# Last token pair of a down projection: the gate row folded into the last product's weight sums

## Chip, core and metric
The kernel runs on one core of one Trainium2 chip. The metric is the device time of one execution in microseconds (us). A core has five engines that run side by side: TensorE (PE, matmuls; PEld is its weight load), VectorE (DVE), ScalarE (ACT), GpSimd (POOL) and SyncE (SP, which here issues the DMAs). Matmul results go to PSUM, in eight banks of 512 f32 columns by 128 partitions; everything else lies in SBUF.

## What is computed
A transformer block on 2048 tokens of width 1024: linear attention, then a gated feed-forward network (hidden width 3584), each with a layer norm that is modulated by a condition vector and each added back through a gate row.

```
x = x + ga * attention(norm(x) * (1 + ca) + sa)
h = norm(x) * (1 + cb) + sb
x = x + gb * ((gelu(h @ w_gate) * (h @ w_up)) @ w_down)
```

The case lies in the last factor: `y @ w_down`, with y of 2048 x 3584, then the gate row gb (1024 numbers, one for each output column) and the sum with x. The output is bf16.

## The kernel before
One Python function records every instruction through a small scheduler (`sch.op`, `sch.dma`), which works out the semaphores from the byte ranges that each instruction reads and writes. Instructions run on each engine in the order in which they were recorded. A reordering by costs (`sch.reorder`) is applied to the part between the two marks, which ends before the down projection: in the part of this case the order is the one written by hand. A write of a range waits for its last TensorE reader, matmul by matmul.

The down projection goes by eight **token pairs** j of 256 tokens. A pair's product is seen as 2 x 2 blocks: token halves s (128 tokens each), halves l of each pair of the 28 hidden chunks, and output halves c (512 columns each). Instead of eight block products it takes **seven**, of sums of blocks (a Strassen-type scheme). Each of the seven is fourteen matmuls (NST = 14, k = 0 to 13): stationary operand 128 x 128 of activations, moving operand 128 x 512 of weights. The weights' sums (`TT[k][0..4]`, tiles named bt) were made once for all pairs, on VectorE (L1585) and ScalarE. The activations' sums (`XS[0]`, `XS[1]`, tiles named xs) are made for each pair from the loaded y (`YL`, tiles named yl): by `a_sum` on VectorE (L1613, in two halves of seven chunks each, `halves(i)`), the last as a copy on ScalarE (L1607).

The order for a pair is product 1, 5, 6, 2, 7, 3, 4 (`dprod`, whose matmuls are all recorded at L1619). Between them:
- `dpcp` (L1653, ScalarE) copies product 1 to bank BB, on which products 6, 7 and 4 are then summed up; `descp` (L1657, ScalarE) copies product 5 to SBUF.
- `halves(0)` must come before product 5, `halves(1)` before 6, `halves(2)` before 7, `halves(3)` before 3, and the copy of L1607 before 4. Products 5, 7 and 4 use XS[0], products 6 and 3 XS[1], so each sum also waits for the product that read the buffer before.
- `dpadd(j, BC)` (L1661, VectorE) reads bank BB after product 6 and before product 7; `dpadd(j, BE)`, after product 7 and before product 4.
- `devac(j, n)` evacuates a finished block n: VectorE multiplies the bank by the gate row GB16 in place (L1684), adds x from the slot `SLT` into the slot (L1685), and SyncE issues the store (L1686). Block 0 is ready after product 2, block 2 after the second `dpadd`, block 1 after product 3, block 3 (second 128 tokens, first 512 columns, bank BB) after product 4. Block 3 of a pair is evacuated during the next pair.

For the last pair, j = 7, nothing follows that could hide the evacuation of block 3. There product 4 covers 448 columns only. The last 64 columns are computed by `plain`, without sums, as 28 matmuls of 64 columns into the other BB bank; the evacuation is then in two parts, 448 and 64 columns, each a multiplication, a sum and a store.

GpSimd has no instruction in the down projection. Its last ones are the 128x1 steps of the second layer norm (L703, L707, L708, L710).

Of the kernel before, what the change touches and what calls it, by code (L numbers as in the profile page):

```python
# [8 lines left out]
ALU = mybir.AluOpType  # L9
# [55 lines left out]
NKP = NFP  # L65
NST = 14
# [30 lines left out]
OFF_SLOT = [OFF_ROW + 2048, OFF_ROW + 3072, OFF_GAB, OFF_GAB + 1024, OFF_GAB + 2048, OFF_GAB + 3072, OFF_GUH + 7168]  # L97
# [251 lines left out]
def bass_adaLN_cond__linear_attn_block__geglu_ffn__prompt_kernel(  # L349
# [18 lines left out]
    with ExitStack() as es:  # L368
# [6 lines left out]
        def at(name, shape, dty, off):  # L375
            return nc.alloc_sbuf_tensor_at(name, shape, dty, offset=ABASE + off, align_bytes=4)
# [21 lines left out]
        GB16 = at("gb16", [P, D], bf16, OFF_GB16)  # L398
        BXT = [at(f"bx{k}", [P, 2, 512], bf16, PB[k]) for k in range(NKP)]
        STT = [at(f"wst{k}", [P, 2, 512], bf16, PS2[k]) for k in range(NKP)]  # L400
        TT = [[at(f"bt{k}_{i}", [P, 512], f32r, PT[k][i]) for i in range(5)] for k in range(NST)]
        SLT = [at(f"x1s{i}", [P, 512], bf16, o) for i, o in enumerate(OFF_SLOT)]
# [59 lines left out]
        def r_sm(name):  # L462
            return [(SMO[name], SMO[name] + SMSZ[name], name)]
# [30 lines left out]
        def r_wv(g):  # L494
            return [(OFF_WK + g * 2048, OFF_WK + (g + 1) * 2048, "wv")]
# [64 lines left out]
        def r_bt(k, i):  # L560
            return [(PT[k][i], PT[k][i] + 2048, f"bt{k}_{i}")]

        def r_slot(i):
            return [(OFF_SLOT[i], OFF_SLOT[i] + 1024, f"x1s{i}")]
# [6 lines left out]
        R_GB16 = [(OFF_GB16, OFF_GB16 + 2048, "gb16")]  # L571
# [4 lines left out]
        def pr(b):  # L576
            return [(b * 2048, (b + 1) * 2048)]

        def PS(b, c0=0, c1=512):
            return ps_all[:, b * 512 + c0: b * 512 + c1]  # L580
# [4 lines left out]
        sch = Sched()  # L585
        T, A, V, G, Q = PE_, ACT_, DVE_, POOL_, SP_
# [3 lines left out]
        out_v = out[0].rearrange("(c p) d -> p c d", p=P)  # L590
# [60 lines left out]
        for q in range(1, 4):  # L651
            wmq_dma(q)
            for d0, d1 in ((2 * q, 2 * q + 1), (2 * q + 1, 2 * q + 2)):
# [8 lines left out]
               rd=r_sm("c8") + r_sm("ident"), pwr=pr(4))  # L662
# [4 lines left out]
               rd=r_sm("thc") + r_sm("chalf"), wr=r_sm("siluT"))  # L667
# [509 lines left out]
        for c_ in range(10, NCH):  # L1177
            b = seq.index(("k", c_ // 2 * 2, 0)) - (9 if c_ % 2 else 12)
# [6 lines left out]
        for c_ in range(8, NCH, 2):  # L1185
            b = seq.index(("k", c_, 0)) - 3
# [10 lines left out]
        for g in range(NG):  # L1197
            task(nk + g // 2, lambda g=g: sch.dma(Q, lambda e: e.dma_start(WV[:, g, :, :], wqkv_v[:, :, 2 * D + g * P:2 * D + (g + 1) * P]),
                                                  wr=r_wv(g), note=f"wv{g}"))
# [246 lines left out]
        BA, BE, BB, BC = 0, 2, 4, 6  # L1446
# [128 lines left out]
        TTF = [[t_.ap().bitcast(f32) for t_ in r_] for r_ in TT]  # L1575
# [23 lines left out]
        def a_sum(i, k0, k1, sh=0):  # L1599
            if k1 <= k0:  # L1600
                return
            lo = lambda s: YL[0][:, k0:k1, s * P:(s + 1) * P]
            hi = lambda s: YL[1][:, k0:k1, s * P:(s + 1) * P]
            x = lambda n: XSF[n][:, k0:k1, :]
            rl, rh = (lambda s: r_yl(0, k0, k1, s * P, (s + 1) * P)), (lambda s: r_yl(1, k0, k1, s * P, (s + 1) * P))
            if i == 4:
                sch.op(A, lambda e: e.activation(XS[0][:, k0 + sh:k1 + sh, :], hi(1), ACTF.Copy), rd=rh(1), wr=r_xq(0, k0 + sh, k1 + sh), note=f"acp.{k0}", overwrite_ok=True)  # L1607
                return
            d, in0, in1, op, rd = ((0, lo(1), hi(1), ALU.add, rl(1) + rh(1)),
                                   (1, x(0), lo(0), ALU.subtract, r_xq(0, k0, k1) + rl(0)),  # L1610
                                   (0, lo(0), lo(1), ALU.subtract, rl(0) + rl(1)),
                                   (1, hi(0), x(1), ALU.subtract, rh(0) + r_xq(1, k0, k1)))[i]
            sch.op(V, lambda e: e.tensor_tensor(XS[d][:, k0:k1, :], in0, in1, op), rd=rd, wr=r_xq(d, k0, k1), note=f"asum{i}.{k0}", overwrite_ok=True)  # L1613
# [13 lines left out]
        def dprod(j, i, k0, k1, n=512):  # L1627
            t, ks = j % 2, range(k0, k1)
            if i in (1, 2):
                lhs = [ya(i - 1, 0, k) for k in ks]  # L1630
                rhs = [(BXT[k][:, i - 1, :], r_bx(k, i - 1, i)) for k in ks]
            else:
                xi, ti = {5: (0, 0), 6: (1, 1), 7: (0, 2), 3: (1, 3), 4: (0, 4)}[i]
                sh = NEA if j == 0 and i == 4 else 0
                lhs = [(XS[xi][:, k + sh, :], r_xq(xi, k + sh, k + sh + 1)) for k in ks]
                rhs = [(TT[k][ti][:, 0:n], r_bt(k, ti)) for k in ks]
            b = {1: BA, 2: BA, 5: BE, 6: BB, 7: BB, 4: BB, 3: BC}[i] + t
            dmm(b, i in (1, 5) and k0 == 0, lhs, rhs, f"down j{j} P{i}", 0, n)

        def plain(j, s, c, k0, k1, b=None, c0=0, c1=512):  # L1640
            if b is None:
                b, fresh = ((BA, BC), (BB, BE))[s][c] + j % 2, False
            else:
                fresh = True
            w = (BXT, STT)[c]
            r = (r_bx, r_st)[c]
            lhs = [ya(l, s, k) for k in range(k0, k1) for l in range(2)]
            rhs = [(w[k][:, l, c0:c1], r(k, l, l + 1)) for k in range(k0, k1) for l in range(2)]
            dmm(b, fresh, lhs, rhs, f"down j{j} C{s}{c}", 0 if fresh else c0, c1 - c0 if fresh else c1)

        def dpcp(j):
            t = j % 2
            sch.op(A, lambda e: e.activation(PS(BB + t), PS(BA + t), ACTF.Copy), prd=pr(BA + t), pwr=pr(BB + t), note="pcp")  # L1653
# [5 lines left out]
        def dpadd(j, dst):  # L1659
            t = j % 2  # L1660
            sch.op(V, lambda e: e.tensor_tensor(PS(dst + t), PS(BB + t), ES[0][:, :], ALU.add), prd=pr(BB + t), rd=r_2k(OFF_ES[0], "es0"),  # L1661
                   pwr=pr(dst + t), note="padd")

        def tok(j):
            return (j // 4) * 8 + 2 * (j % 4)

# [9 lines left out]
        def devac(j, n, c0=0, c1=512, b=None):  # L1676
            s, c = TORD[n]
            i, c_ = (4 * j + n) % 7, tok(j) + s
            if b is None:
                b, p0, p1 = ((BA, BC), (BB, BE))[s][c] + j % 2, c0, c1  # L1680
            else:
                p0, p1 = 0, c1 - c0
            rng = [(OFF_SLOT[i] + c0 * 2, OFF_SLOT[i] + c1 * 2, f"x1s{i}")]
            sch.op(V, lambda e: e.tensor_tensor(PS(b, p0, p1), PS(b, p0, p1), GB16[:, c * 512 + c0:c * 512 + c1], ALU.mult), prd=pr(b), pwr=pr(b), rd=R_GB16, note=f"x2a {j}.{n}")  # L1684
            sch.op(V, lambda e: e.tensor_tensor(SLT[i][:, c0:c1], PS(b, p0, p1), SLT[i][:, c0:c1], ALU.add), prd=pr(b), rd=rng, wr=rng, note=f"x2b {j}.{n}")  # L1685
            sch.dma(Q, lambda e: e.dma_start(out_v[:, c_, c * 512 + c0:c * 512 + c1], SLT[i][:, c0:c1]), rd=rng, note=f"out{c_}.{c}.{c0}")  # L1686

        mark.append(sch.n)
        def cb1():
# [42 lines left out]
        for n in range(8):  # L1732
            i, j = divmod(n, 2)
# [4 lines left out]
        for n in range(4 * NEA):  # L1738
            v, k = 14 + (n + 1) // 2, (7, 1)[n % 2]
# [35 lines left out]
        def halves(i):  # L1775
            a_sum(i, 0, H)
            a_sum(i, H, NST)
# [40 lines left out]
        for j in range(1, NP):  # L1818
            lastj = j == NP - 1
            dprod(j, 1, 0, NST)  # L1820
            dpcp(j)
            if j == 1:
                devac(0, 0)
            else:
                halves(0)
                halves(1)
                devac(j - 1, 3)
            x1_load(j, 3)
            dprod(j, 5, 0, NST)
            descp(j)  # L1830
            halves(2)
            if not lastj:
                y_load(j + 1, 0)
            if j == 1:
                devac(0, 1)
            dprod(j, 6, 0, NST)
            dpadd(j, BC)
            halves(3)
            if j == 1:
                devac(0, 2)  # L1840
            dprod(j, 2, 0, NST)
            devac(j, 0)
            if not lastj:
                x1_load(j + 1, 0)
            dprod(j, 7, 0, NST)
            dpadd(j, BE)
            a_sum(4, 0, H)
            if not lastj:
                y_load(j + 1, 1, 0, H)
            a_sum(4, H, NST)  # L1850
            if not lastj:
                y_load(j + 1, 1, H, NKP)
            devac(j, 2)
            if j == 1:
                devac(0, 3)
            if not lastj:
                x1_load(j + 1, 1)
            dprod(j, 3, 0, NST)
            devac(j, 1)
            if not lastj:  # L1860
                x1_load(j + 1, 2)
            if not lastj:
                dprod(j, 4, 0, NST)
            else:
                dprod(j, 4, 0, NST, 448)
                plain(j, 1, 0, 0, NKP, b=BB + 1 - j % 2, c0=448, c1=512)
                devac(j, 3, 0, 448)
                devac(j, 3, 448, 512, b=BB + 1 - j % 2)


        sch.reorder(mark[0], mark[1], (DVE_, ACT_, POOL_), {id(x4_op): 8.0})
# [73 lines left out]
```

## Time and profile before

| what | us |
|---|---|
| median of 3 runs (lowest, highest) | 786.57 (786.21, 787.83) |
| the profiled execution | 786.67 |
| its span, first to last instruction | 784.9 |
| PE busy | 777.6 (99%) |
| DVE busy | 644.6 (82%) |
| ACT busy | 347.3 (44%) |
| POOL busy | 44.5 (6%) |
| last pair's matmuls (product 1 to the 64 column piece) | 759.14 to 781.84 |
| last DMA issue | 782.90 to 783.29 |

Times "at" are counted from the span's start. The granted TensorE clock is 1.00 over the whole span. Busy shares are means over stages; the change lies in the last 3% of the span, so its own stretch has to be read. A matmul's length in the trace includes its way through the array, and matmuls overlap: the distance from start to start is what one costs.

### The profile page before, as it was taken

The page shows a single profiled execution, that of the slowest core. Times are in us where ns is not written, and L with a number is a line of the kernel's source. Part 1 is how long each engine was busy: PE and PEld are TensorE (multiplying, and loading weights), DVE is VectorE, ACT ScalarE, POOL GpSimd, SP SyncE. Part 2 cuts the span into 40 slices and gives each one's busy share as a digit, 9 for nine tenths or more (in the row PEclk, how much of TensorE's full clock was granted, in tenths as well). Part 3 has the DMA queues.
Part 4 walks back from the last instruction along what each step waited for, and adds up shares of the span by engine and source line. Part 5 has one row for each costly group of instructions (what it writes and reads, how often), then busy time and mean ns, then how long its engine had stood idle before and what let it go on. Part 6 is the DMA issues. An engine that isn't in the chain of part 4 may idle for free.

```text
span 784.9 us, 11098 instructions
## 1 busy us (share of the span) xinstructions
PE 777.6 (99%) x3897; PEld 498.7 (64%) x3897; DVE 644.6 (82%) x1082; ACT 347.3 (44%) x584; POOL 44.5 (6%) x126
## 2 busy tenths in 40 slices
PE   8999999999999999999999999999999999999998
PEld 4444445666445667677777767677776576777766
DVE  6699989993498987888999988898988897676775
ACT  2497743333474476766645444444545011111111
POOL 2031300000230011010000000000000000000000
PEclk9999999999999999999999999999999999999999
DMA  9789749826596377555455567555536445344341
GB/s 283 254 168 249 158 93 255 220 69 115 134 256 188 90 230 236 155 148 148 120 145 170 143 182 207 162 162 150 153 100 182 123 127 162 119 141 138 111 141 35
DMA packets 210544, 125.94 MB, mean 160 GB/s; under 512 B 70572, under 2 KB 200116, under 8 KB 210488
## 3 DMA queue, kind: packets, MB, share of 16 engines
q1 hardware_dynamic: 210472, 125.23, 58.8%
q8 instruction: 31, 0.51, 0.3%
q14 instruction: 25, 0.20, 0.1%
q10 hardware_dynamic: 16, 0.00, 0.0%
HBM read 88.35 MB, written 23.22 MB: 142 GB/s over the span
## 4 chain that ended last, share of the span: by engine, by line
PE 94%; DMA 3%; SPq 2%; DVE 1%; issue 0%; ACT 0%; DVEq 0%; ACTq 0%
PE ps_all L1468 45%; PE ps_all L1619 23%; PE ps_all L1303 7%; PE ps_all L969 7%; PE ps_all L933 6%; PE ps_all L918 5%; DMA mtb<-mb 1%; DMA wmq<-in_w_mod_dram 1%; SPq L631 1%; SPq L636 0%; DMA h1T<-xh 0%; PE ps_all L951 0%; PE ps_all L1234 0%; PE ps_all L1261 0%; SPq L625 0%
## 5 line engine op out<-in xcount | busy, mean ns | idle before, releaser
L1468 PE MATMUL ps_all<-ss,tp 128*128 128x512 f32 x896 | 224.9, 403 | 0.0
L1468 PEld LDWEIGHTS ps_all<-ss,tp 128*128 128x128 f32 x896 | 167.8, 188 | 41.1 <-DVE ps_all L1480 0.7
L1485 ACT ACTIVATE ge<-ps_all 128x512 f32<-128x512 f32 x112 | 66.8, 597 | 133.1 <-DVE ps_all L1480 82.3
L1619 PE MATMUL ps_all<-bt,xs 128*128 128x512 f32 (+1 forms) x520 | 123.8, 395 | 0.0
L1619 PEld LDWEIGHTS ps_all<-bt,xs 128*128 128x128 f32 x520 | 97.6, 188 | 22.2 <-DVE ps_all L1661 0.5
L1489 DVE TENSOR_TENSOR yr<-ge,ps_all 128x512 bf16<-128x512 f32 x112 | 76.7, 685 | 30.5 <-PE ps_all L1468 14.4
L1480 DVE TENSOR_TENSOR ps_all<-ps_all,es 128x512 f32<-128x512 f32 x112 | 72.4, 692 | 7.8 <-PE ps_all L1468 6.9
L1442 DVE TENSOR_TENSOR tp<-wt 128x512 fp32r<-128x512 bf16 x112 | 72.1, 685 | 1.3
L1442 DVE TENSOR_TENSOR tp<-wt,tp 128x512 fp32r<-128x512 bf16 x112 | 72.1, 685 | 0.0
L1619 PE MATMUL ps_all<-bx,yl 128*128 128x512 bf16 (+1 forms) x268 | 58.2, 360 | 0.0
L918 PE MATMUL ps_all<-wk,h1T 128*128 128x512 bf16 x248 | 56.9, 379 | 0.4 <-DVE h1T L758 0.2
L969 PE MATMUL ps_all<-h1T,wq 128*128 128x512 bf16 x256 | 56.7, 379 | 0.0
L1303 PE MATMUL ps_all<-w,pq 128*128 128x512 bf16 x256 | 56.4, 379 | 0.0
L1468 PE MATMUL ps_all<-ar,tp 128*128 128x512 f32 x224 | 55.3, 389 | 0.0
L1468 PE MATMUL ps_all<-h21a,wt 128*128 128x512 bf16 x224 | 53.2, 380 | 0.0
L1468 PE MATMUL ps_all<-h20a,wt 128*128 128x512 bf16 x224 | 53.0, 380 | 0.0
L907 ACT ACTIVATE eb<-ps_all 128x512 f32<-128x512 f32 x64 | 36.3, 593 | 37.0 <-PE ps_all L918 15.7
L1468 PEld LDWEIGHTS ps_all<-ar,tp 128*128 128x128 f32 x224 | 42.1, 188 | 8.7
L969 PEld LDWEIGHTS ps_all<-h1T,wq 128*128 128x128 bf16 x256 | 25.0, 98 | 29.9
L1303 PEld LDWEIGHTS ps_all<-w,pq 128*128 128x128 bf16 x256 | 24.8, 98 | 30.3 <-issue 0.5
L1474 ACT ACTIVATE ps_all<-ps_all 128x512 f32<-128x512 f32 x56 | 32.6, 582 | 21.8 <-PE ps_all L1468 16.8
L918 PEld LDWEIGHTS ps_all<-wk,h1T 128*128 128x128 bf16 x248 | 23.5, 98 | 29.1 <-DVE h1T L758 2.5
(147 smaller groups left out, 888.0 us busy)
## 6 DMA issues: line engine op xcount, KB each, us to landing
wt<-in_B_w_gate_dram SPq DMA_DIRECT2D x28, 512.0 KB, 4.0
wt<-in_B_w_up_dram SPq DMA_DIRECT2D x28, 512.0 KB, 5.0
scr_y<-yr SPq DMA_DIRECT2D x56, 256.0 KB, 2.7
yl<-scr_y SPq DMA_DIRECT2D x8, 896.0 KB, 4.5
wmst<-in_w_mod_dram SPq DMA_DIRECT2D x6, 1024.0 KB, 5.6
yl<-scr_y SPq DMA_DIRECT2D x12, 448.0 KB, 4.3
wmq<-in_w_mod_dram SPq DMA_DIRECT2D x8, 512.0 KB, 6.2
rb<-scr_rd SPq DMA_DIRECT2D x32, 128.0 KB, 3.0
```

What stands on the lines that cost most here:

```text
L907: sch.op(A, lambda e: e.activation(EB[i][:, :], PS(bank), ACTF.Exp), prd=pr(bank), wr=rng, note=f"{note}.exp")
L918: o = sch.op(T, lambda e, dc=dc: e.matmul(PS(bank), H1[sg][:, ci, dc, :], W_[:, dc, jg * 512:(jg + 1) * 512], start=(dc == 0), stop=(dc == ...
L933: o = sch.op(T, lambda e, c_=c_: e.matmul(PS(bank, 0, n), PK[c_][:, g * P:(g + 1) * P], xrow(c_, o_, o_ + n), start=(c_ == 0), stop=(c_ == ...
L969: o = sch.op(T, lambda e, dc=dc: e.matmul(PS(b), WQ[:, dc, qc * P:(qc + 1) * P], H1[sg][:, :, dc, :], start=(dc == 0), stop=(dc == NDC - 1 ...
L1303: last[half] = sch.op(T, lambda e, g=g, half=half: e.matmul(PS(b0 + half), PQ[sg][:, g, ci * P:(ci + 1) * P], W2[:, g, half * 512:(half + ...
L1442: sch.op(V, lambda e, t=t: e.tensor_tensor(TP[k][:, t, :, :], in0[:, t, :, :], in1[:, t, :, :], ALU.subtract), rd=r0[t:t + 1] + (r1[t:t + ...
L1468: o = sch.op(T, lambda e, l_=l_, r_=r_, dc=dc: e.matmul(PS(b), l_, r_, start=fresh and dc == 0, stop=dc == ND2 - 1, skip_group_check=True) ...
L1474: sch.op(A, lambda e: e.activation(PS(BB + t), PS(BA + t), ACTF.Copy), prd=pr(BA + t), pwr=pr(BB + t), note="pcp")
L1480: sch.op(V, lambda e: e.tensor_tensor(PS(dst + t), PS(BB + t), ES[t][:, :], ALU.add), prd=pr(BB + t), rd=r_2k(OFF_ES[t], f"es{t}"), pwr=pr ...
L1485: sch.op(A, lambda e: e.activation(GE[i][:, :], PS(b), ACTF.Gelu_apprx_tanh), prd=pr(b), wr=r_2k(OFF_GE[i], f"ge{i}"), note="gelu")
L1489: sch.op(V, lambda e: e.tensor_tensor(YR[:, 2 * (v % 2) + l, h * SGW:(h + 1) * SGW], GE[i][:, :], PS(b + 1), ALU.mult), rd=r_2k(OFF_GE[i], ...
L1619: pend_ = sch.op(T, lambda e, l_=l_, r_=r_, i=i: e.matmul(PS(b, c0, c1), l_, r_, start=fresh and i == 0, stop=i == n - 1, skip_group_check ...
```

## The change
All of it concerns the last pair only.
- The 64 column piece is gone; product 4 covers all 512 columns.
- The weight sums of product 4, `TT[k][4]` (128 x 512 f32, SBUF), are multiplied by the first half of the gate row (bf16, SBUF) in place: k = 0 to 8 on GpSimd, recorded after product 1; k = 9 to 11 on VectorE behind `halves(2)` and ahead of the first `dpadd`; k = 12 and 13 on VectorE behind `devac(7, 0)`. They wait for pair 6's product 4, which reads the same sums without the gate.
- When bank BB has been read by the second `dpadd`, VectorE multiplies what it holds by the gate row and adds x, both in the bank (`rest_gate`), ahead of product 4, which is then summed on top.
- After product 4 the bank is copied out as it is, in two halves of 256 columns, each with its own store (`last_out`).

Line numbers below L1664 move by 3 to 24: L1684 to L1686 become L1687 to L1689, the gates are L1665. L1613, L1619 and L1661 keep theirs.

```
+        def t4_gate(k, eng):
+            sch.op(eng, lambda e: e.tensor_tensor(TT[k][4][:, :], TTF[k][4][:, :], GB16[:, 0:512], ALU.mult), rd=r_bt(k, 4) + R_GB16, wr=r_bt(k, 4), note=f"t4g{k}")
...
+        def rest_gate(j):
+            b, i = BB + j % 2, (4 * j + 3) % 7
+            sch.op(V, lambda e: e.tensor_tensor(PS(b), PS(b), GB16[:, 0:512], ALU.mult), prd=pr(b), pwr=pr(b), rd=R_GB16, note="u3g")
+            sch.op(V, lambda e: e.tensor_tensor(PS(b), PS(b), SLT[i][:, :], ALU.add), prd=pr(b), pwr=pr(b), rd=r_slot(i), note="u3x")
+
+        def last_out(j):
+            b, i, c_ = BB + j % 2, (4 * j + 3) % 7, tok(j) + 1
+            for p0, p1 in ((0, 256), (256, 512)):
+                rng = [(OFF_SLOT[i] + p0 * 2, OFF_SLOT[i] + p1 * 2, f"x1s{i}")]
+                sch.op(V, lambda e, p0=p0, p1=p1: e.tensor_copy(SLT[i][:, p0:p1], PS(b, p0, p1)), prd=pr(b), wr=rng, note="last")
+                sch.dma(Q, lambda e, p0=p0, p1=p1: e.dma_start(out_v[:, c_, p0:p1], SLT[i][:, p0:p1]), rd=rng, note=f"out{c_}.0.{p0}")
...
             dpcp(j)
+            if lastj:
+                for k in range(9):
+                    t4_gate(k, G)
...
             halves(2)
+            if lastj:
+                for k in range(9, 12):
+                    t4_gate(k, V)
...
             devac(j, 0)
+            if lastj:
+                for k in range(12, NST):
+                    t4_gate(k, V)
...
             dpadd(j, BE)
+            if lastj:
+                rest_gate(j)
...
             else:
-                dprod(j, 4, 0, NST, 448)
-                plain(j, 1, 0, 0, NKP, b=BB + 1 - j % 2, c0=448, c1=512)
-                devac(j, 3, 0, 448)
-                devac(j, 3, 448, 512, b=BB + 1 - j % 2)
+                dprod(j, 4, 0, NST)
+                last_out(j)
```

## The prediction
> **What bounds the kernel now.** I read the shares of the span first, then the chain that ended last, then the last token pair in order of time.
>
> ```profile
> PE   8999999999999999999999999999999999999998
> DVE  6699989993498987888999988898988897676775
> POOL 2031300000230011010000000000000000000000
> ```
>
> One digit is a fortieth of the span (19.6 us). TensorE is full to the end, VectorE has a few tenths free near the end, GpSimd does nothing in the second half. The chain is TensorE without a break up to 781.02, then VectorE:
>
> ```profile
> 734.99 46.03 PE ps_all L1619 x206
> ...
> 781.04 0.64 DVE ps_all L1684
> ...
> 781.78 0.62 DVE x1s L1685
> 782.40 0.15 DVE ps_all L1684
> ...
> 782.58 0.22 DVE x1s L1685
> ```
>
> So a gain must shorten what follows TensorE's last matmuls, and anything that delays TensorE in the last pair (759.14 to 781.84) is paid in full. VectorE in that pair (start, length, what ended the idle time before):
>
> ```profile
> 757.85 1.09 DVE L1613 TENSOR_TENSOR xs<-yl,yl 128x896 fp32r<-128x896 bf16 x1 [0.19 <-PE ps_all L1619]
> 759.43 1.09 DVE L1613 TENSOR_TENSOR xs<-yl,yl 128x896 fp32r<-128x896 bf16 x1 [0.49 <-PE ps_all L1619]
> 760.44 2.09 DVE L1613 TENSOR_TENSOR xs<-xs,yl 128x896 fp32r<-128x896 f32 x2
> ...
> 765.60 1.09 DVE L1613 TENSOR_TENSOR xs<-yl 128x896 fp32r<-128x896 bf16 x1 [0.51 <-PE ps_all L1619]
> 768.84 0.70 DVE L1661 TENSOR_TENSOR ps_all<-ps_all,es 128x512 f32<-128x512 f32 x1 [2.15 <-PE ps_all L1619]
> 769.45 2.08 DVE L1613 TENSOR_TENSOR xs<-yl,xs 128x896 fp32r<-128x896 bf16 x2
> ```
>
> The activation sums (L1613) come about 3 us before TensorE uses them, and the free places are 2.15 us before the first L1661 and 1.73 us before the second (775.03).
>
> **The end: what is removed.** Product 4's fourteen matmuls start at 778.00; at 448 columns they follow each other every 0.203 us and the last (780.64, 0.37 long) ends at 781.01. The 28 narrow matmuls that go (780.85 to 781.84) lay beside VectorE's 448 column gate and sum (781.04 to 782.40), so taking them away gives nothing by itself. What goes from the path is VectorE's four instructions: 781.04 to 782.80, then SyncE's last issue at 782.90.
>
> **What replaces it.** At 512 columns matmuls follow every 0.227 us (774.83 to 777.78, fourteen of product 3): the last starts at 778.00 + 13 x 0.227 = 780.95, ends 0.39 later at 781.34, and the first copy starts at 781.38. A copy of 256 columns out of PSUM is not in the trace. The cast of 256 columns at L1268, from SBUF, took 290 ns; 256 columns out of PSUM at L1266 took 425, and L1685's 224 ns at 64 and 625 at 448 columns give the same 425. I take 0.425, the row that reads PSUM. It ends at 781.80, its DMA issue starts 0.07 later (as 782.40 to 782.48 before), takes 0.33, and the second issue follows at 782.30; the second copy has ended by 782.15. That is 0.60 us before 782.90 (0.74 with copies of 0.29). The last transfer grows from 16 KB to 64 KB: before, 16 KB were done 1.5 us after their issue, 112 KB after 1.7, so up to 0.2 is given back. The end is worth **-0.5 us** (-0.4 to -0.7).
>
> **The work that moves ahead of product 4, if nobody disturbs anybody.** VectorE's gates k = 9 to 11 cost 3 x 0.685 = 2.06 (the subtractions of L1442 and L1585 have the same shape and two SBUF inputs) in the 2.15 us free; gates 12 and 13 cost 1.37 in 1.73. The two instructions on the rest of the bank (L1684's 0.70 and about 0.8 with its gap) lie at 775.75 to 777.3, before product 4's 778.00, and push product 3's and 5's evacuations back by 0.8 to 1.5, to about 779.8, before 781.38. All this costs nothing, with margins of 0.09, 0.36 and 0.7 us. No DMA is issued earlier or later but the last ones. GpSimd's nine gates may start when pair 6's product 4 lets go of its sums one by one: that starts at 755.96, so the first at 756.4. The ninth is due at 778.00 + 8 x 0.227 = 779.8: alone on its engine GpSimd may take 2.6 us for each. Sum so far: 786.67 - 0.5.
>
> **One gate on GpSimd.** The trace has no wide two-input operation there. Bounds: its memset of 256 columns took 317 ns against 99 for one column (0.85 ns a column, writing only): 0.19 + 511 x 0.85 = 0.63 us, with the 0.19 of a 128x1 operation. Its L612, 128 columns with one input, took 568: if all above 0.19 is by the column, 2.97 ns, so 1.71 us; with two inputs at that price each 3.2. L612's fixed part may be larger (L708's 128x1 takes 566 whatever its length), so I take the middle of 0.63 and 1.71, **1.2 us**. The Trainium skill (GPSIMD Engine Reference, 3.1 Elementwise) has about 2.6 cycles an element for two inputs: by it, as an estimate, 1.1 us and a start, which would take up to 1 us off the sum below.
>
> **The cost that the diff does not show.** GpSimd and VectorE get in each other's way. In order of time, start and length, then one line by its source:
>
> ```profile
> 224.99 1.29 DVE L1442 TENSOR_TENSOR tp<-wt,tp 128x512 fp32r<-128x512 bf16 x2
> 225.06 0.66 POOL L707 TENSOR_SCALAR ve<-st 128x1 f32<-128x1 f32 x1 [1.48 <-ACT xl L705]
> ...
> 226.19 1.29 DVE L1295 TENSOR_TENSOR pq<-pq,rb 128x1024 bf16<-128x1024 bf16 x2
> 226.78 0.75 POOL L710 TENSOR_TENSOR nm<-mv,rs 128x1 f32<-128x1 f32 x1
> ```
> ```profile
> L710 POOL TENSOR_TENSOR nm<-mv,rs x25: 191/191/1141, 39.8 to 364.0; 128x1 f32<-128x1 f32 x25
> ```
>
> L707 and L710 take 0.19 us as a rule (the last line: least, median, most). Beside VectorE operations whose two inputs both lie in SBUF they take 0.66 and 0.75, and end 0.05 us after such an operation ends (225.67, 227.48). At 274 to 276 us, beside L1489, one of whose inputs is in PSUM, they take 0.19. L707 at 225.06 came through between two VectorE operations that follow without a pause: the two engines **take turns**. That VectorE waits likewise for GpSimd the trace cannot show, since every GpSimd operation here is tiny. Bounds: no wait at all, or GpSimd's whole operation. I take the second, because GpSimd's own wait lasted to the end of VectorE's operation. The Trainium skill (SBUF — State Buffer, Who interferes with whom) says so outright: VectorE with two SBUF inputs and a GpSimd operation that reads SBUF exclude each other for a whole instruction, whoever comes first. The trace agrees for one direction (0.75 for 0.19); no run yet shows the other.
>
> What then happens, with turns of 1.2 us for GpSimd and 1.0 for a half of L1613: the second gate holds until 758.9, so the first half of L1613 starts at 758.9 instead of 757.85; the next three at 761.1, 763.3 and 765.5 (759.43, 760.44, 761.45), each behind another gate; pair 6's evacuation has one input in PSUM and runs beside the sixth gate; the next halves at 769.0 and 771.2; the ninth gate ends at 773.45, VectorE's three gates at 775.45, and L1661, queued behind them, starts there instead of at 768.84. Product 7 may not write the bank that L1661 reads: it starts at 776.1 instead of 771.42, **4.7 us late**. VectorE is now the bound: two halves (2.0), an evacuation (1.55), two gates (1.3), L1661 (0.75), two on the rest (1.6), to 783.3, and product 4 starts there instead of at 778.00: **+5.3 us**. Each 0.1 us on GpSimd's operation adds 0.9 (0.63 us: +0.3; 1.71 us: +9.8).
>
> **Forecast:** 786.67 + 5.3 - 0.5 = **791.5 us**. This stands against the profiled execution, which lies 0.1 above the median of the runs, 786.57; that is left in.
>
> **Rivals.**
> - *VectorE does not wait for GpSimd* (it gets its inputs whatever GpSimd reads; only GpSimd waits). For it: no VectorE operation in the trace is longer beside GpSimd (L1442 keeps its 685 ns). Against: those GpSimd operations are too short to show it. Then GpSimd has until 779.8 and only the end counts: 786.67 - 0.5 = 786.2, not slower. It decides as long as a gate, its own waits included, stays under 2.6 us; with 12 us of two-input VectorE work in that stretch to wait for, 1.2 us just fits.
> - *GpSimd keeps its turn until its nine are through* (the next gate starts before VectorE gets in). Then L1613 starts after 756.4 + 9 x 1.26 = 767.7 and the same sum gives +7.2: 793.4. Against: L707 came in between two operations.
> - *Gates so cheap (0.63 to 0.8 us) that slack takes most of the wait*: +0.3 to +1.7, 786.5 to 787.9.
> - *The change does not do what it says*: the order of instructions has the narrow matmuls gone and nine gates on GpSimd; it does.
>
> **How the numbers follow.** Turns: 0.58; GpSimd keeps its turn: 0.12; VectorE does not wait: 0.26; cheap gates: 0.04. A measurement of this kernel can tell about 0.2%, 1.6 us, from no change. Faster by more than that would need three times the end's gain: 0.02. Within: 0.27. Slower: 0.71. The likeliest case alone reaches from 788.8 (0.9 us a gate) to 796.0 (1.7). With the undisturbed case in, 785.9 to 796.0; gates above 1.7 us and the longest waits stay out.
>
> **What would show it.** Right: in the last pair L1613's operations are longer than 1.09 us or stand idle with GpSimd running, the first L1661 starts near 775, TensorE stands still before products 7 and 4, GpSimd's gates are near 1.2 us with gaps of 1.0. Wrong: L1613 keeps its 1.09 us and starts, TensorE runs through, and the last issue comes 0.6 us after product 4's copy as worked out. Wrong in size: another length of the gate, 0.9 us for each 0.1.

## The result, and the profile after
The changed kernel takes 789.65 us (median of 5 runs, 788.54 to 790.08) where the kernel before took 786.45 (785.83 to 787.83): ratio **1.0039, interval 1.0028 to 1.0050**, 3.2 us slower. 791.5 was forecast; 789.65 lies in the range that was given. The profiled execution took 789.65 us, with a span of 787.9.

GpSimd's nine gates, then VectorE in the last pair, in order of time (start, length, count at the end):

```profile
755.72 15.20 POOL L1665 TENSOR_TENSOR bt<-bt,gb 128x512 fp32r<-128x512 f32 x9 [392.10 <-PE ps_all L1619]
```
```profile
757.07 3.85 DVE L1613 TENSOR_TENSOR xs<-yl,yl 128x896 fp32r<-128x896 bf16 x2 [0.19 <-PE ps_all L1619]
760.83 4.02 DVE L1613 TENSOR_TENSOR xs<-xs,yl 128x896 fp32r<-128x896 f32 x2
...
766.17 3.73 DVE L1613 TENSOR_TENSOR xs<-yl 128x896 fp32r<-128x896 bf16 x2
769.83 2.84 DVE L1665 TENSOR_TENSOR bt<-bt,gb 128x512 fp32r<-128x512 f32 x3
772.60 0.69 DVE L1661 TENSOR_TENSOR ps_all<-ps_all,es 128x512 f32<-128x512 f32 x1
773.20 2.08 DVE L1613 TENSOR_TENSOR xs<-yl,xs 128x896 fp32r<-128x896 bf16 x2
```

VectorE has no idle time from 757.1 to 777.8. The first six halves of L1613 take 1.8 to 2.05 us each where they took 1.09; the last two, after GpSimd has finished (at 770.92), are back at 1.08. L1661 starts at 772.60. This execution's last pair began 0.78 us earlier than that of the profiled execution before (product 1 at 758.36, not 759.14), so in the times of before that is 773.38, against 768.84. The same by source line (least, median, most in ns), first L1613 in the window 756.9 to 770, then the gates:

```profile
L1613 DVE TENSOR_TENSOR xs<-yl,yl x2: 1881/1960/2039, 757.1 to 758.9; 128x896 fp32r<-128x896 bf16 x2
```
```profile
L1665 POOL TENSOR_TENSOR bt<-bt,gb x9: 1161/1998/2017, 755.7 to 768.9; 128x512 fp32r<-128x512 f32 x9
L1665 DVE TENSOR_TENSOR bt<-bt,gb x5: 678/682/1636, 769.8 to 777.2; 128x512 fp32r<-128x512 f32 x5
```

A wait for the other engine shows as a longer operation and not as idle time: GpSimd's gate is 1.16 us undisturbed and 2.0 beside L1613, VectorE's gate 0.68 and, once, 1.64.

TensorE, then its granted clock by stretch (length, busy time and count, clock; the last two figures are the DMA engines' share and GB/s):

```profile
767.79 3.20 PE L1619 MATMUL ps_all<-bx,yl 128*128 128x512 bf16 x13
773.34 11.46 PE L1619 MATMUL ps_all<-bt,xs 128*128 128x512 f32 x42 [2.35 <-DVE ps_all L1661]
```
```profile
773.30:774.60 1.30, 1.26 (x5) 1.00 0.00 0
774.60:778.00 3.40, 3.40 (x10) 0.53 0.12 39
778.00:781.00 3.00, 3.00 (x14) 0.97 0.01 2
```

TensorE stands still for 2.35 us until L1661 is done, and 1.4 us after it has started again its clock falls to a half for 3.4 us: 42 matmuls take 11.46 us. The kernels of E1 to E3 below, with the same 42 matmuls and the clock at 1.00, take 9.92. So the fall costs **1.5 us** more. It comes in some executions only: of the five, those at a mean clock of 1.000 took 788.54 and 788.63 us, those at 0.997 to 0.998 took 789.65, 790.07 and 790.08.

The end:

```profile
784.83 0.76 DVE L1700 CAST x1s<-ps_all 128x256 bf16<-128x256 f32 x2 [1.36 <-PE ps_all L1619]
785.33 0.81 SPq L1701 DMA_DIRECT2D out_dram<-x1s  x2
```

From the first copy to the end of the span 3.07 us pass (784.83 to 787.9); before, from the first instruction of the last evacuation, 3.86 (781.04 to 784.9). Less the 0.34 us by which product 4 is longer, the new end gains 0.45 us.

### The profile page after: what moved, and what is told of

Its sections match the earlier page's. It is cut to its first block, busy times and chain, and to the rows that moved or that the text cites. A ratio compares the mean times of both kernels' runs of the same rounds, so it can differ in the third digit from the quotient of the medians.

```text
span 787.9 us, 11003 instructions
## 1 busy us (share of the span) xinstructions
PE 774.7 (98%) x3806; PEld 499.0 (63%) x3869; DVE 653.5 (83%) x1087; ACT 347.2 (44%) x584; POOL 59.3 (8%) x135
## 4 chain that ended last, share of the span: by engine, by line
PE 91%; SPq 3%; DMA 3%; DVE 2%; issue 1%; ACT 0%; DVEq 0%; ACTq 0%
PE ps_all L1468 44%; PE ps_all L1619 21%; PE ps_all L969 7%; PE ps_all L1303 7%; PE ps_all L933 6%; PE ps_all L918 5%; SPq L631 1%; DMA mtb<-mb 1%; DVE xs L1613 1%; SPq L636 1%; DMA wk<-in_A_wqkv_dram 1%; PE ps_all L951 0%; DMA h1T<-xh 0%; DVE bt L1665 0%; PE ps_all L1234 0%
## 5 line engine op out<-in xcount | busy, mean ns | idle before, releaser
L1619 PE MATMUL ps_all<-bt,xs 128*128 128x512 f32 x520 | 125.7, 400 | 2.4 <-DVE ps_all L1661 2.4
L1619 PEld LDWEIGHTS ps_all<-bt,xs 128*128 128x128 f32 x520 | 98.7, 190 | 25.5 <-DVE ps_all L1661 3.2
L1489 DVE TENSOR_TENSOR yr<-ge,ps_all 128x512 bf16<-128x512 f32 x112 | 76.7, 685 | 30.5 <-PE ps_all L1468 14.5
L1619 PE MATMUL ps_all<-bx,yl 128*128 128x512 bf16 x227 | 56.0, 380 | 0.7
L918 PE MATMUL ps_all<-wk,h1T 128*128 128x512 bf16 x239 | 55.3, 379 | 1.2 <-DMA wk<-in_A_wqkv_dram 0.7
L1468 PE MATMUL ps_all<-h21a,wt 128*128 128x512 bf16 x210 | 50.0, 380 | 1.0
L1468 PE MATMUL ps_all<-h20a,wt 128*128 128x512 bf16 x210 | 50.0, 380 | 0.9
L1665 POOL TENSOR_TENSOR bt<-bt,gb 128x512 fp32r<-128x512 f32 x9 | 15.2, 1724 | 392.1 <-PE ps_all L1619 392.1
```

The costliest lines, as they stand in the source:

```text
L918: o = sch.op(T, lambda e, dc=dc: e.matmul(PS(bank), H1[sg][:, ci, dc, :], W_[:, dc, jg * 512:(jg + 1) * 512], start=(dc == 0), stop=(dc == ...
L1468: o = sch.op(T, lambda e, l_=l_, r_=r_, dc=dc: e.matmul(PS(b), l_, r_, start=fresh and dc == 0, stop=dc == ND2 - 1, skip_group_check=True) ...
L1489: sch.op(V, lambda e: e.tensor_tensor(YR[:, 2 * (v % 2) + l, h * SGW:(h + 1) * SGW], GE[i][:, :], PS(b + 1), ALU.mult), rd=r_2k(OFF_GE[i], ...
L1619: pend_ = sch.op(T, lambda e, l_=l_, r_=r_, i=i: e.matmul(PS(b, c0, c1), l_, r_, start=fresh and i == 0, stop=i == n - 1, skip_group_check ...
```

## The experiments
The theory after the result: six halves of L1613 wait for GpSimd's gates and use up the slack that VectorE had, then the three VectorE gates ahead of L1661 have no idle time left to lie in, and the whole queue reaches TensorE; the pause then brings its clock down. Rivals: VectorE's added instructions alone are too many; GpSimd's turns alone reach TensorE; the clock fell for another reason. Each ratio is to the kernel before on the same chip (785.88 us for E1 to E4, 786.07 for E5 to E8).

**E1, without GpSimd's gates.**
```
             dpcp(j)
-            if lastj:
-                for k in range(9):
-                    t4_gate(k, G)
```


> The changed kernel with GpSimd's nine gates left out (the sums k = 0 to 8 of the last product stay ungated, so a part of the last block is not the reference's); VectorE's five gates, the rest gate and the two copies stay. Theory, turns: product 7 was 2.7 us late because six halves of L1613 waited for GpSimd and the three VectorE gates behind them had no idle time left. Then here L1613 is back to 1.09 us, the first L1661 starts right after product 6, TensorE does not pause, its clock is 1.000, and only the shorter end is left: 786.45 - 0.55 = 785.9. Rival, VectorE's own load: the seven added VectorE instructions alone delay TensorE; then it stays near 788.5 to 789.6.

Measured: 785.41 us, ratio 0.9991 (0.9982 to 1.0000).
```profile
765.97 1.89 DVE L1665 TENSOR_TENSOR bt<-bt,gb 128x512 fp32r<-128x512 f32 x3
768.20 0.70 DVE L1661 TENSOR_TENSOR ps_all<-ps_all,es 128x512 f32<-128x512 f32 x1 [0.35 <-PE ps_all L1619]
```
The three gates take 1.89 us in the free place, L1661 waits for product 6 as before, and TensorE does not pause. VectorE's seven added instructions cost nothing by themselves; that rival falls.

**E2, without VectorE's gates.**
```
             halves(2)
-            if lastj:
-                for k in range(9, 12):
-                    t4_gate(k, V)
...
             devac(j, 0)
-            if lastj:
-                for k in range(12, NST):
-                    t4_gate(k, V)
```


> The changed kernel with VectorE's five gates left out (k = 9 to 13 stay ungated, a part of the last block is not the reference's); GpSimd's nine stay where they are. Theory, turns that eat slack: L1613 still takes 1.8 to 2.05 us for six halves, but without the three gates in the queue (2.8 us in the changed kernel) the first L1661 starts near 770 instead of 772.6, before product 7 needs it: no pause, clock 1.000, 785.9. Rival, GpSimd's turns alone reach TensorE: a pause before product 5, 6 or 7 remains, 787 to 789.

Measured: 785.15 us, ratio 0.9990 (0.9981 to 0.9999).
```profile
765.69 3.73 DVE L1613 TENSOR_TENSOR xs<-yl 128x896 fp32r<-128x896 bf16 x2
769.34 0.69 DVE L1661 TENSOR_TENSOR ps_all<-ps_all,es 128x512 f32<-128x512 f32 x1
```
```profile
767.30 3.20 PE L1619 MATMUL ps_all<-bx,yl 128*128 128x512 bf16 x13
770.15 9.92 PE L1619 MATMUL ps_all<-bt,xs 128*128 128x512 f32 x42
```
L1613 is as long as in the changed kernel (3.73 us for two), yet product 7 starts on time at 770.15, with L1661 done 0.12 us earlier, at 770.03. So GpSimd's turns alone cost nothing either, but they leave nothing over. In the kernel before, VectorE is through with `halves(2)` at 766.69, and L1661 need not start before 770.67 (product 7's 771.42, less L1661's 0.70, less the 0.05 that lie between the two in the changed kernel): a slack of 4.0 us. Here `halves(2)` ends at 769.42, which is 770.69 in the times of before (product 1 starts 1.27 us earlier here): the turns take all 4.0. The three gates of E1 take 1.9 of the same 4.0. **Neither part costs anything; the two together make product 7 2.7 us late**, because both spend the same slack.

**E3, the gates apart.** All fourteen are made, but GpSimd's beside VectorE work that reads PSUM.
```
                 halves(1)
+                if lastj:
+                    for k in range(2):
+                        t4_gate(k, G, [sch.streams[V][-1]])
...
             halves(2)
             if lastj:
-                for k in range(9, 12):
+                for k in range(2, 7):
                     t4_gate(k, V)
...
             halves(3)
+            if lastj:
+                for k in range(7, NST):
+                    t4_gate(k, G, [sch.streams[V][-1]])
```
(The last argument is the VectorE instruction that the gate waits for; the two other places are gone.)

> All fourteen gates are made, at other places: GpSimd's k = 0 and 1 behind the second activation sum (beside an evacuation with an input in PSUM), VectorE's k = 2 to 6 behind the third, GpSimd's k = 7 to 13 behind the fourth (beside VectorE work that reads PSUM only). Theory, turns: GpSimd's gates take 1.16 us, no L1613 is longer than 1.09 us but the one after the first two gates, the first L1661 starts near 770 and ends before product 7's 771.4, the last gate ends near 780.6 where product 4's last matmul wants it at 780.95: no pause, 785.9. Rival, any work of GpSimd beside VectorE costs, or VectorE's five gates in a row delay L1661: a pause of 1 us or more, 787 or more.

Measured: 785.75 us, ratio 0.9995 (0.9987 to 1.0004).
```profile
L1665 POOL TENSOR_TENSOR bt<-bt,gb x9: 1173/1183/1197, 761.7 to 778.4; 128x512 fp32r<-128x512 f32 x9
```
```profile
L1613 DVE TENSOR_TENSOR xs<-yl x2: 1078/1472/1867, 763.0 to 764.8; 128x896 fp32r<-128x896 bf16 x2
```
GpSimd's nine gates now all take 1.17 to 1.20 us, the last seven beside VectorE work with an input in PSUM, and only the half of L1613 that meets the second gate is long (1.87), as expected. TensorE runs through (42 matmuls in 9.92 us). The 3.2 us are gone. That it beats the kernel before is not shown: the end's gain of half a microsecond is under 0.1%, and the interval holds 1.

**E4, E5 and E6, the pause by itself.** The kernel before, with GpSimd idle and n VectorE operations on an unused PSUM bank ahead of L1661 (n = 9, 12 and 7):
```
+            if lastj:
+                for _ in range(9):
+                    sch.op(V, lambda e: e.tensor_tensor(PS(BB), PS(BB), GB16[:, 0:512], ALU.mult), prd=pr(BB), pwr=pr(BB), rd=R_GB16, note="idle")
             dpadd(j, BC)
```


> The kernel before, with nine multiplications of an unused PSUM bank put on VectorE ahead of the last pair's first L1661; GpSimd idle, the end as before. This makes product 7 late by itself, by about 2.7 us (766.7 + 9 x 0.75, then L1661's 0.7, against 771.42). Theory, the pause has a price of its own: with the granted clock at 1.000 it costs 2.7 us, 789.2; in some executions the clock falls by half for 3.4 us after the pause, as in the profiled execution of the changed kernel, and these take 1.5 us more, 790.6 at a mean clock of 0.998. Rival, the fall of the clock came from GpSimd or from the gates: 789.2 in every execution, clock 1.000.

> As the run with the pause only, with twelve multiplications instead of nine: product 7 about 4.6 us late. Theory, a pause of TensorE brings the clock down when it is long enough, by a chance that grows with its length (in 3 of 5 executions of the changed kernel with 2.35 us, in 1 of 7 with 2.05): here the clock falls in every execution, 4.6 + 1.5 = 6.1 above before, 792. Rival, the fall has nothing to do with the pause's length: 4.6 above before in most executions, 790.5, a fall in a few.

> As above with seven multiplications: product 7 about 0.9 us late. Theory: the clock stays at 1.000 in every execution, 0.9 above before, 786.8. Rival, as above: a fall in one execution of five or so.

TensorE's row behind the pause in E4, E5 and E6 in turn:
```profile
772.64 11.10 PE L1619 MATMUL ps_all<-bt,xs 128*128 128x512 f32 x42 [2.05 <-DVE ps_all L1661]
```
```profile
775.94 11.07 PE L1619 MATMUL ps_all<-bt,xs 128*128 128x512 f32 x42 [4.25 <-DVE ps_all L1661]
```
```profile
772.02 9.52 PE L1619 MATMUL ps_all<-bt,xs 128*128 128x512 f32 x42 [0.58 <-DVE ps_all L1661]
```
| kernel | pause | time, ratio (interval) | executions with mean clock 0.998 or less |
|---|---|---|---|
| E6, n = 7 | 0.58 | 787.11, 1.0011 (1.0002 to 1.0020) | 0 of 11 |
| E4, n = 9 | 2.05 | 788.24, 1.0027 (1.0016 to 1.0038) | 1 of 7 |
| changed kernel | 2.35 | 789.65, 1.0039 (1.0028 to 1.0050) | 3 of 5 |
| E5, n = 12 | 4.25 | 792.67, 1.0084 (1.0071 to 1.0098) | 5 of 5 |

E4 brings most of the loss back without GpSimd and without a gate. Product 7 is 2.4 us late there (2.7 were expected); six of its executions took 787.79 to 788.88 us, and the one with the fall, the profiled one, 789.47. E5 and E6 came out as expected, with the fall in every execution and in none. The fall follows the pause, more often the longer it is. The counts are small, and so low a mean clock also stood in 2 of 108 executions of kernels without a pause (E1 to E3, E7, E8 and the runs of before beside them), where it was not profiled; that E4's fall belongs to the pause is read from its profile, where it lies right behind it.

Why the same pause brings the clock down in some executions only can be read from the ten profiles. In each of them, from the first change on record, the clock changes only at whole multiples of 3.413 us. The first change lies at 6.78 us in the changed kernel, 8.12 in E4 and 5.15 in E5; the falls come at 774.78, 772.70 and 776.56, which is 225, 224 and 226 such steps later. Where the steps lie differs from execution to execution, and what TensorE did within one step decides on the next. Around the falls in the changed kernel, E4 and E5, then behind E4's last matmuls:
```profile
771.37:774.78 3.41, 1.44 (x6) 1.00 0.00 0
774.78:778.19 3.41, 3.41 (x9) 0.50 0.12 41
```
```profile
769.29:772.70 3.41, 1.31 (x7) 1.00 0.01 2
772.70:776.12 3.42, 3.42 (x8) 0.50 0.00 0
```
```profile
769.74:773.15 3.41, 1.90 (x9) 1.00 0.00 0
773.15:776.56 3.41, 0.62 (x3) 1.00 0.00 0
776.56:779.98 3.42, 3.42 (x10) 0.50 0.00 0
```
```profile
782.94:786.36 3.42, 1.63 (x32) 1.00 0.21 68
786.36:787.60 1.24, 0.00 (x0) 1.00 0.13 24
```
In all ten profiles the clock fell after every step in which matmuls took 1.44 us or less, and after none with 1.63 or more. (Most of these steps hold the last matmuls of a kernel, where a fall costs nothing; in the kernel before the clock falls there too, at 784.24.) So between 1.8 and 2.0 us of idle time have to lie within one step. By that, as an estimate, a pause of 2.05 or 2.35 us brings a fall in about half of the executions, according to where the steps lie, one under 1.8 us in none and one of 4.25 us in all; 1 of 7, 3 of 5, 0 of 11 and 5 of 5 fit this as far as such small counts can.

**E7, GpSimd only writes.** Each of GpSimd's gates is replaced by two memsets of the same sums.
```
-                    t4_gate(k, G)
+                    sch.op(G, lambda e, k=k: e.memset(TTF[k][4][:, :], 0.0), wr=r_bt(k, 4), note=f"ms{k}", overwrite_ok=True)
+                    sch.op(G, lambda e, k=k: e.memset(TTF[k][4][:, :], 0.0), wr=r_bt(k, 4), note=f"ms{k}b", overwrite_ok=True)
```


> The changed kernel with each of GpSimd's nine gates replaced by two memsets of the same sums to zero (128 x 512, written, nothing read; the last block is then not the reference's), with the same waits; about 18 x 0.6 = 11 us of GpSimd work at the same place, VectorE's five gates stay. Theory, the two engines take turns over reads of SBUF: L1613 keeps 1.09 us, no pause, 785.3 as without GpSimd's gates. Rival, any SBUF work of GpSimd holds VectorE's two-input operations back: L1613 is longer than 1.09 us again and the time is 787 or more.

Measured: 785.84 us, ratio 0.9999 (0.9990 to 1.0008). GpSimd's work lies from 755.99 to 765.5, 0.53 us for each memset.
```profile
L1613 DVE TENSOR_TENSOR xs<-yl,yl x2: 1093/1093/1093, 757.4 to 759.0; 128x896 fp32r<-128x896 bf16 x2
L1613 DVE TENSOR_TENSOR xs<-xs,yl x2: 1084/1085/1086, 760.0 to 761.0; 128x896 fp32r<-128x896 f32 x2
```
L1613 does not notice it, and TensorE does not pause. (The time is 0.5 us above the 785.3 that was expected; the interval just reaches down to that.) GpSimd's being at work, its waits and its writes are not what holds VectorE back; what is left of the gate, by exclusion, is its reading of SBUF. The Trainium skill (SBUF — State Buffer, Who interferes with whom) says this: two SBUF inputs on VectorE collide with GpSimd's reads, not with an operation that only writes. These rows agree.

**E8, the last store on a second queue**, in the kernel of E3.
```
-                sch.dma(Q, lambda e, p0=p0, p1=p1: ...
+                sch.dma(A if p0 else Q, lambda e, p0=p0, p1=p1: ...
```


> The kernel with the gates apart, and its last store issued by ScalarE's queue instead of SyncE's. Theory: SyncE's two last issues follow each other (the second waits for the first, 0.1 us after its copy is there), so 0.1 us earlier than with one queue, 785.6 where that was 785.75; both 0.1% or less under before. Rival: ScalarE's issue is slower or its store lands later: 785.8 or more.

Measured: 786.04 us, ratio 0.9998 (0.9989 to 1.0007). In the profile 2.96 us pass from the first copy to the end (780.64 to 783.6), 2.98 in E3 (780.42 to 783.4). Nothing that can be told apart: the 0.1 us that was expected is not to be seen.

## Why the prediction was right, and where its sizes were off
- *The two engines take turns, and VectorE waits for GpSimd's whole operation*: right, L1613 went from 1.09 to 2.04 us. That was the direction which the trace of before could not show, and the whole forecast hung on it. The rival in which VectorE does not wait (0.26) falls, and so does the one in which GpSimd keeps its turn until its nine are through: halves and gates alternate.
- *One gate, 1.2 us*: 1.16 to 1.20.
- *A turn* was mis-sized. I added GpSimd's 1.2 and VectorE's 1.0, 2.2 us a round. Measured: two of GpSimd's gates from 756.84 take 3.12 us and three take 5.08, so a round is 1.96, over 0.2 less. The ninth gate ended at 770.92, in the times of before 771.70, where 773.45 was worked out, 1.75 us sooner; from there VectorE's three gates took 1.7 more instead of 2.0, and L1661 came at 773.38 (in the times of before) instead of 775.45.
- *Product 7 late by 4.7 us*: 2.7 (773.34 + 0.78 against 771.42), for these two reasons. The place, L1661 behind the three gates, was right.
- *VectorE the bound up to product 4, +5.3 in all*: +4.2 in the profiled execution (the first copy at 784.83 + 0.78 against the 781.38 worked out without a pause). But 1.5 of that is the clock, which I had not thought of. TensorE did not stand still before product 4, as the prediction had it: VectorE waited 0.56 us for product 7, so it was not the bound there. That hung on the clock as well. In E1 the second L1661 starts 3.61 us after product 7 (774.39 against 770.78), which here would have been 776.95, and VectorE was busy until 777.88; with the clock at 1.00 product 4 would have been late by about 0.4 us (an estimate from these rows; no execution of the changed kernel without the fall was profiled). Errors of opposite sign, 2 us too much for the turns, 0.6 too much for a wait before product 4 that did not come, and 1.5 too little for the clock, brought the sum nearer than its working deserved. The range helped too: at 785.9 to 796.0 it held the case in which nothing is lost as well, so it is the lengths and starts in the trace that bear the mechanism out, not the time.
- *The end, -0.5*: 0.45. The copy of 256 columns out of PSUM took 425 ns, as taken from the rows for PSUM and not the 290 of the cast.
- *One row was misread.* At 274.57 L707 ran while VectorE was idle (its L1489 had ended at 274.05 and the next began at 274.94), so only L710 at 275.49 lay beside an operation with an input in PSUM. The conclusion holds by E3, where seven wide gates beside such work keep their 1.2 us.
- *Nothing lost if nobody disturbs anybody*, with margins of 0.09, 0.36 and 0.7 us: E1 shows it. What I did not see is that GpSimd's turns fit into the slack as well, if the three gates are elsewhere (E2), so that the cost is one of the combination.

In sum, in the times of before: 2.7 for the pause, 1.5 for the clock, less 0.45, is 3.75. The profiled spans differ by 3.0, since the later execution's pair happened to begin 0.78 earlier.

## What to carry to other kernels
Slack can be spent once. GpSimd's turns (six long operations) and three extra gates each fitted into the 4 us that VectorE was ahead; both together did not, and a row for each alone shows neither. In these runs work given to GpSimd cost VectorE time only where VectorE read two operands from SBUF and GpSimd read too: put such work beside VectorE work on PSUM (E3), and look for the wait in the length of the operations, not in their idle time. A pause of TensorE of some 2 us or more is to be priced with a possible 1.5 us on top, in about half of the executions at 2 us and in all of them at 4.25.

## What the runs showed of the hardware
- After a pause of TensorE of 2.05 to 4.25 us the granted clock fell to a half, for 3.4 us in the profiles, while matmuls were following each other again: 0.43 us from start to start instead of 0.23. It changed only in steps of 3.413 us, and fell after a step with 1.44 us or less of matmuls in it, not after one with 1.63 or more. The Trainium skill (TensorE: Matmul & The Clock Gate, Part 1) has such a window of 3413 ns and the half rate, which agrees, but lets the clock fall after at least one idle window of about 3.4 us; here 2.05 and 2.35 us were enough in 1 of 7 and 3 of 5 executions. By that rule the changed kernel would have taken 788.6 in every execution, as the two without a fall did.
- VectorE and GpSimd alternate even where both have more work ready: a round of 1.96 us, although the two operations alone take 1.16 and 1.09.
